# A seven-slot K ring, half-size softmax steps and a turned down projection in a two-layer decode kernel

## The chip, the cores and the metric

The kernel runs on one core of one Trainium2 chip. The metric is the device time of one execution in microseconds (us).

PE is the tensor engine, DVE the vector engine, ACT the scalar engine, SP the engine that only issues the loads here. PSUM is the memory that PE writes to; the kernel uses it as eight banks of 512 float32 columns per partition.

## The reference

One token per sequence is decoded (batch 4, model width 512). The same attention layer and the same feed-forward layer are applied twice, with the same weights and the same caches. Shortened:

```python
# x: (4, 1, 512); k_cache, v_cache: (4, 8, 8192, 128); 32 query heads, 8 K/V heads
# wq: (512, 4096)   wo: (4096, 512)   w_gate, w_up: (512, 1792)   w_down: (1792, 512)   all bfloat16
def attention(x):
    q = (x @ wq).reshape(4, 1, 32, 128).transpose(0, 2, 1, 3)
    k = jnp.repeat(k_cache, 4, axis=1)
    v = jnp.repeat(v_cache, 4, axis=1)
    p = softmax(einsum("bhqd,bhkd->bhqk", q, k) * 128 ** -0.5)
    o = einsum("bhqk,bhkd->bhqd", p, v)
    return o.transpose(0, 2, 1, 3).reshape(4, 1, 4096) @ wo

def ffn(x):
    return (silu(x @ w_gate) * (x @ w_up)) @ w_down

for layer in range(2):                     # written out in the reference
    x = x + attention(layernorm(x))
    x = x + ffn(layernorm(x))
```

## The kernel before

Per layer there are 64 K chunks and then 64 V chunks, each 1 MB: 1024 positions of one K/V head for all four sequences. A K chunk is loaded by SP, transposed by PE in 32 blocks of 128x128 into PSUM "staging" banks, copied out by DVE or ACT, and multiplied with the padded queries (`qk`). After every eight chunks (a range of 1024 positions for all heads) DVE takes a maximum and ACT an exponential. When all 64 chunks are through, `finalize_pt` brings the eight ranges to one common maximum and transposes P; then the V chunks are multiplied (`pv`).

Three things in it matter for the change. The first is where K chunks lie. Four buffers (`kraw`) form a ring. Chunks 4, 5 and 6 lie in the three V buffers, and transposing those releases no load:

```python
    NSK = 4
    NSV = 3
    ...
        VK = (4, 5, 6)
        ring_chunks = [i for i in range(nchunks) if i not in VK]
        NRING = NSK

        def kslot(i):
            if i in VK:
                j = i - VK[0]
                return vbuf[:, j, :, :], f"vb{j}", sem_v[j]
            r = ring_chunks.index(i) % NRING
            if r < NSK:
                return kraw[:, r, :, :], f"kraw{r}", sem_k[r]
            ...
        def ring_next(i):          # the load that transposing chunk i makes possible
            if i in VK:
                return None
            r = ring_chunks.index(i) + NRING
            return ring_chunks[r] if r < len(ring_chunks) else None

        vslot_aps = [vbuf[:, j, :, :] for j in range(NSV)] + wqr_aps   # V: three buffers, then the quarters of wq_sb
```

The second is the use of the PSUM banks. Two pairs hold scores in turn (a pair is a whole range), which leaves four banks for staging:

```python
        stgK_x = [0, 1, 2, 7]
        sc_banks = [["pb3", "pb4"], ["pb5", "pb6"]]
        ...
            def softmax_range(c):          # once per eight chunks
                j = c % 2
                T.op("dve", lambda e: e.tensor_reduce(negm[:, c:c + 1], sc[j][:, :], AX.X, ALU.max, negate=True), ...)
                T.op("act", lambda e: e.activation(pp[:, c * SR:(c + 1) * SR], sc[j][:, :], ACTF.Exp,
                                                   bias=negm[:, c:c + 1], scale=1.0, accum_out=lsum[:, c:c + 1]), ...)
            ...
            def k_loop():
                for i in range(HEAD - 1):
                    qk(i)
                for i in range(HEAD, nchunks):
                    transposes(i)
                    qk(i - 1)
                qk(nchunks - 1)
```

The third is the layer boundary, whose order of issue is also the order of work on PE (in the trace from 369.38 us, the transposes of chunk 0, to 390.25, the Q projection), and the down projection in it:

```python
        def ffn_down():
            for fo in range(FO):                       # 14 matmuls of 512 columns, four rows of output
                bank = MISC - (fo % 2)
                T.op("pe", lambda e: e.matmul(ps[0:B, bank * BANKF:(bank + 1) * BANKF],
                                              lhsT=hT[:, fo * B:(fo + 1) * B], rhs=wd_sb[:, fo, :], ...), ...)

        def ffn_residual():
            for bank in (MISC, MISC - 1):
                T.op("dve", lambda e: e.tensor_tensor(x_sb[:], x_sb[:], ps[0:B, bank * BANKF:(bank + 1) * BANKF], ALU.add), ...)
        ...
        L1["pv"](next_layer=L2)
        L2["prefetch_vk"]()
        ev0 = L2["transposes"](0, banks=[0, 1, 2, 4], defer_evac=True)
        L1["residual"]()
        ffn_up()
        ev0()
        ffn_act(final=False)
        ffn_down()
        ev1 = L2["transposes"](1, banks=[3, 5, 0, 1], defer_evac=True)
        ffn_residual()
        L2["qproj"]()
```

One oddity concerns both kernels alike. Wq is loaded once, V chunks then overwrite its four quarters, and layer 2's Q projection multiplies with what lies there. (The program has a line that loads Wq again, but under `if not last`, which is false for layer 2, the only layer that calls it.) The result still passes the comparison with the reference; why it passes was not tested.

Of the kernel before, what the change touches and what calls it, by code (L numbers as in the profile page):

```python
# [5 lines left out]
ALU = mybir.AluOpType  # L6
# [96 lines left out]
def bass_interleave_layers__gqa_block_cached__swiglu_ffn__decode_kernel(  # L103
# [24 lines left out]
    NCH = S // SR  # L128
    NSK = 4
# [6 lines left out]
    with ExitStack() as es:  # L136
# [24 lines left out]
        negm = sb("negm", [P, NCH], FP32)  # L161
        lsum = sb("lsum", [P, NCH], FP32)
        gnegm = sb("gnegm", [P, 1], FP32)
        dm = sb("dm", [P, NCH], FP32)
        alpha = sb("alpha", [P, NCH], FP32)
        wl = sb("wl", [P, NCH], FP32)
# [8 lines left out]
        hT = sb("hT", [P, FO * B], BF16)  # L175
        xo_bf = sb("xo_bf", [B, D], BF16)
# [9 lines left out]
        stgK = [0, 1, 2]  # L186
        stgK_x = [0, 1, 2, 7]
        stgP = [4, 5, 6]
        sc = [ps[:, 3 * BANKF:5 * BANKF], ps[:, 5 * BANKF:7 * BANKF]]
        sc_banks = [["pb3", "pb4"], ["pb5", "pb6"]]  # L190
# [33 lines left out]

        def act_preload(func):
            T.op("act", lambda e: e.activation(dmy_out[:], dmy_in[:], func), reads=["dmyin"], writes=["dmy"])
# [8 lines left out]
        VK = (4, 5, 6)  # L235
        assert len(VK) <= NSV
        ring_chunks = [i for i in range(nchunks) if i not in VK]

# [3 lines left out]
        NRING = NSK  # L242

        def kslot(i):
            if i in VK:
                j = i - VK[0]
                return vbuf[:, j, :, :], f"vb{j}", sem_v[j]
            r = ring_chunks.index(i) % NRING
            if r < NSK:
                return kraw[:, r, :, :], f"kraw{r}", sem_k[r]  # L250
            j = r - NSK
            return wqr_aps[j], wqr_keys[j], sem_wqr[j]

        def ring_pos(i):
            return None if i in VK else ring_chunks.index(i)

        def ring_next(i):
            if i in VK:
                return None
            r = ring_chunks.index(i) + NRING  # L260
            return ring_chunks[r] if r < len(ring_chunks) else None
# [7 lines left out]
        vslot_aps = [vbuf[:, j, :, :] for j in range(NSV)] + wqr_aps  # L269
        vslot_keys = [[f"vb{j}"] for j in range(NSV)] + [[k] for k in wqr_keys]  # L270
        vsems = sem_v + sem_wqr
# [39 lines left out]
        def make_attention(first, last):  # L311
# [12 lines left out]
            def qproj():  # L324
                layer_norm_T()
# [19 lines left out]
            def transposes(i, banks=None, defer_evac=False):  # L345
# [38 lines left out]
                if nxt == nchunks - 1:  # L384
# [3 lines left out]
                    for v in range(min(nvs, nchunks)):  # L388
                        dma_v(v)

            def softmax_range(c):
                j = c % 2
                T.op("dve", lambda e: e.tensor_reduce(negm[:, c:c + 1], sc[j][:, :], AX.X, ALU.max,  # L393
                                                      negate=True),
                     reads=sc_banks[j], writes=[f"negm{c}"])
                blocks = [f"pp{c * M + m}" for m in range(M)]
                T.op("act", lambda e: e.activation(pp[:, c * SR:(c + 1) * SR], sc[j][:, :], ACTF.Exp,  # L397
                                                   bias=negm[:, c:c + 1], scale=1.0,
                                                   accum_out=lsum[:, c:c + 1]),
                     reads=sc_banks[j] + [f"negm{c}"], writes=blocks + ["lsum"])  # L400

            def qk(i):
                c, g = chunk_coords(i)
                j = c % 2
                for q2 in range(2):
                    for b in range(B):
                        src, skeys = kpiece(i, b)
                        T.op("pe", lambda e: e.matmul(sc[j][32 * b:32 * (b + 1), q2 * 512:(q2 + 1) * 512],  # L408
# [5 lines left out]
                             reads=["qpad"] + skeys, writes=[sc_banks[j][q2]])  # L414
                if g == G - 1:
                    softmax_range(c)

            def k_wq_slots_start():
# [244 lines left out]
```

## Time and profile before

| | before |
|---|---|
| median of the first 6 runs | 748.56 us (747.12 to 750.14) |
| span of the profiled run | 747.0 us |
| read from HBM | 282.33 MB |
| rate in steady stretches | 407 GB/s |
| last V load landed | 725.14 us |

These lines are from the page of the kernel before: the span, the bytes moved in 40 equal slices of it (18.7 us each), the queue of instruction fetches (packets, MB, share), the sum of the reads, and two of the DMA issues (times issued, KB each, median us to landing).

```profile
span 747.0 us, 21812 instructions
...
GB/s 340 406 340 405 388 404 404 393 402 387 395 408 407 407 406 407 406 407 407 410 396 264 279 401 404 405 406 402 400 405 397 407 407 406 408 407 406 407 257 1
...
q8 instruction: 78, 1.28, 0.6%
...
HBM read 282.33 MB, written 0.00 MB: 378 GB/s over the span
...
wq_sb<-in_A_v_cache_dram SPq DMA_DIRECT2D x72, 1024.0 KB, 13.6
...
wq_sb<-in_A_wq_dram SPq DMA_DIRECT2D x1, 4096.0 KB, 17.3
```

Most slices stand at 402 to 408 GB/s, so the load queue is what bounds the kernel nearly all the time. The exceptions are the third slice (340), the two at the layer boundary (264 and 279), and the end. The last two lines are the oddity of Wq: loaded once, with 72 V chunks put into the same tile.

The next lines are the table by stretch of the kernel before. The columns are the stretch and its length, the busy time (and instructions) of PE, PE's weight loads, DVE, ACT and POOL, then the granted PE clock, the share of the DMA engines and GB/s.

```profile
40.00:50.00 10.00, 9.37 (x154) 7.08 (x152) 7.49 (x11) 6.69 (x8) 0.00 (x0) 1.00 0.90 306
...
400.00:410.00 10.00, 8.29 (x139) 6.20 (x140) 5.73 (x13) 3.79 (x4) 0.00 (x0) 1.00 0.66 225
410.00:420.00 10.00, 9.37 (x154) 7.08 (x152) 7.89 (x12) 7.02 (x8) 0.00 (x0) 1.00 0.52 182
420.00:430.00 10.00, 9.72 (x159) 7.54 (x160) 6.14 (x10) 5.92 (x6) 0.00 (x0) 1.00 1.01 355
```

PE is busy for 8.3 to 9.7 us of each ten while the loads stand half still. There the loads wait for PE: in this program a load can only be issued when a buffer has been transposed (SP waited for PE's transposes 257.8 us in all, in 108 waits).

Why PE is late at the boundary is told by the chain of waits of the kernel before (start, duration, what).

```profile
361.69 19.67 DMA wd_sb<-in_B_w_down_dram
381.45 4.80 PE ps L576 x13
...
390.25 3.45 PE ps L328 x128
```

The load of w_down lands at 381.4 us, the down projection takes 4.8 us, and the Q projection of layer 2 can start at 390.25 us.

How fast PE gets through K is seen in the timeline of the kernel before around one softmax (start, duration, engine, line, operation; in brackets the idle time before it and what ended it).

```profile
417.81 1.11 ACT L397 ACTIVATE pp<-ps,negm 128x1024 bf16<-128x1024 f32 x1 [0.91 <-PE ps L359]
...
418.82 0.19 ACT L397 ACTIVATION_READ_ACCUMULATOR pp<-ps,negm 128x1 f32 x1
418.91 1.02 ACT L285 ACTIVATE ktp<-ps 128x1024 bf16<-128x1024 bf16 x1
...
419.98 0.73 PE L359 MATMUL ps<-ident,kraw 128*128 128x128 bf16 x10 [0.63 <-ACT ktp L285]
```

The exponential and its accumulator hold ACT for 1.2 us (417.81 to 419.01); the copy that ACT owes is late; PE has no free staging bank and stops 0.63 us (0.8 us with its weight load). Eight chunks take PE 7 x 2.44 + 3.25 = 20.33 us.

The end of the kernel before, from the timeline:

```profile
725.19 1.04 PE L506 MATMUL ps<-vbuf,pp 128*32 128x128 bf16 x32 [3.03 <-DMA vbuf<-in_A_v_cache_dram]
...
737.87 5.98 PE L576 MATMUL ps<-wd_sb,hT 128*4 128x512 bf16 x14 [1.64 <-DVE hT L571]
743.62 1.39 DVE L583 TENSOR_TENSOR x_sb<-x_sb,ps 4x512 f32<-4x512 f32 x2 [5.80 <-PE ps L576]
```

### The profile page before, as it was taken

Reading aid. Unit: us, or ns where it says so; the run is one execution under the profiler, and the core shown is the slowest. Engines: PE = TensorE matmul, PEld = TensorE weight load, DVE = VectorE, ACT = ScalarE, POOL = GpSimd, SP = SyncE. Lnnn points to the kernel's source line nnn. Section 1 sums busy time; section 2 is a strip of 40 time slices with the busy share of each in tenths; the row PEclk is TensorE's granted clock in tenths of the full one; section 3 lists DMA queues with packets and bytes.
Section 4 is the critical chain, followed back from the end, with each engine's and each line's share of the span. In section 5 each row is a group of like instructions: output and inputs, shape, how many; then the busy total and the mean of one; then the engine's idle time right before and its main releaser. Section 6 shows DMA issues by size and latency. Waiting matters only on the chain.

```text
span 747.0 us, 21812 instructions
## 1 busy us (share of the span) xinstructions
PE 517.6 (69%) x9948; PEld 383.0 (51%) x9948; DVE 278.9 (37%) x466; ACT 232.4 (31%) x258; POOL 1.6 (0%) x11
## 2 busy tenths in 40 slices
PE   3899999999544454444568999999995544445435
PEld 2776777777432333333446777777775333333322
DVE  3376676667500000000234767666664000000002
ACT  3365666566500000000133665656654000000001
POOL 0000000000000000000000000000000000000000
PEclk9799999999855555555578999999998555555555
DMA  8999999999999999999997799999999999999960
GB/s 340 406 340 405 388 404 404 393 402 387 395 408 407 407 406 407 406 407 407 410 396 264 279 401 404 405 406 402 400 405 397 407 407 406 408 407 406 407 257 1
DMA packets 142780, 283.75 MB, mean 380 GB/s; under 512 B 4184, under 2 KB 10080, under 8 KB 142176
## 3 DMA queue, kind: packets, MB, share of 16 engines
q1 hardware_dynamic: 142688, 282.35, 98.7%
q8 instruction: 78, 1.28, 0.6%
q14 instruction: 14, 0.11, 0.0%
HBM read 282.33 MB, written 0.00 MB: 378 GB/s over the span
## 4 chain that ended last, share of the span: by engine, by line
DMA 41%; PE 27%; SPq 21%; DVE 4%; issue 3%; ACT 2%; ACTq 0%; DVEq 0%
SPq L92 21%; PE ps L359 17%; DMA kraw<-in_A_k_cache_dram 15%; DMA wq_sb<-in_A_v_cache_dram 12%; DMA vbuf<-in_A_v_cache_dram 9%; PE ps L408 4%; DMA wd_sb<-in_B_w_down_dram 3%; DMA wq_sb<-in_A_wq_dram 2%; PE ps L506 2%; PE ps L488 2%; DVE negm L393 1%; ACT ktp L285 1%; PE ps L576 1%; PE ps L328 1%; DVE o_red L475 1%
## 5 line engine op out<-in xcount | busy, mean ns | idle before, releaser
L359 PEld LDWEIGHTS ps<-ident,kraw 128*128 128x128 bf16 x3904 | 224.2, 99 | 79.0 <-DMA kraw<-in_A_k_cache_dram 61.6
L359 PE MATMUL ps<-ident,kraw 128*128 128x128 bf16 x3904 | 247.5, 222 | 22.2 <-DMA kraw<-in_A_k_cache_dram 13.2
L283 DVE COPY ktp<-ps 128x1024 bf16<-128x1024 bf16 x310 | 206.7, 688 | 100.4 <-PE ps L359 99.8
L285 ACT ACTIVATE ktp<-ps 128x1024 bf16<-128x1024 bf16 x186 | 183.5, 1021 | 119.7 <-PE ps L359 119.7
L506 PE MATMUL ps<-wq_sb,pp 128*32 128x128 bf16 x2304 | 77.5, 300 | 85.4 <-DMA wq_sb<-in_A_v_cache_dram 84.6
L475 DVE TENSOR_REDUCE o_red<-ps 128x128 f32<-128x384 f32 x16 | 8.9, 557 | 298.3 <-PE ps L506 298.3
L506 PEld LDWEIGHTS ps<-wq_sb,pp 128*32 128x32 bf16 x2304 | 57.0, 132 | 104.1 <-DMA wq_sb<-in_A_v_cache_dram 93.0
L297 ACT ACTIVATE sdv<-mv,eps_sb 4x1 f32<-4x1 f32 x4 | 1.2, 293 | 338.7 <-DVE mv L296 338.7
L506 PE MATMUL ps<-vbuf,pp 128*32 128x128 bf16 x1792 | 58.7, 292 | 65.6 <-DMA vbuf<-in_A_v_cache_dram 65.6
L506 PEld LDWEIGHTS ps<-vbuf,pp 128*32 128x32 bf16 x1792 | 42.8, 129 | 80.2 <-DMA vbuf<-in_A_v_cache_dram 72.4
L408 PE MATMUL ps<-ktp,qpad 128*32 128x512 bf16 x992 | 76.4, 384 | 3.8 <-DVE qpad L340 3.4
L488 PE MATMUL ps<-wo_sb,oT_sb 128*4 128x512 bf16 x64 | 29.9, 621 | 5.1 <-DVE oT_sb L486 5.1
L408 PEld LDWEIGHTS ps<-ktp,qpad 128*32 128x32 bf16 x992 | 15.6, 94 | 17.7 <-DVE qpad L340 3.8
L397 ACT ACTIVATE pp<-ps,negm 128x1024 bf16<-128x1024 f32 x16 | 17.8, 1113 | 18.2 <-DVE negm L393 15.5
L393 DVE TENSOR_REDUCE negm<-ps 128x1 f32<-128x1024 f32 x16 | 19.6, 1224 | 6.9 <-PE ps L408 6.9
L283 DVE COPY pp<-ps 128x1024 bf16<-128x1024 bf16 x20 | 13.4, 688 | 20.6 <-PE ps L359 17.3
L285 ACT ACTIVATE pp<-ps 128x1024 bf16<-128x1024 bf16 x12 | 12.1, 1023 | 20.3 <-PE ps L359 16.4
L460 PE MATMUL ps<-ident,pp 128*128 128x128 bf16 x128 | 11.6, 273 | 8.1 <-DVE pp L451 7.9
L483 PE MATMUL ps<-ident,o_accb 128*128 128x128 bf16 x16 | 4.6, 288 | 16.7 <-DVE o_accb L480 14.8
L460 PEld LDWEIGHTS ps<-ident,pp 128*128 128x128 bf16 x128 | 10.8, 127 | 9.6 <-DVE pp L451 8.9
L576 PE MATMUL ps<-wd_sb,hT 128*4 128x512 bf16 x28 | 11.0, 575 | 5.3 <-DMA wd_sb<-in_B_w_down_dram 3.6
L488 PEld LDWEIGHTS ps<-wo_sb,oT_sb 128*4 128x4 bf16 x64 | 5.6, 108 | 17.5 <-issue 9.5
(58 smaller groups left out, 114.1 us busy)
## 6 DMA issues: line engine op xcount, KB each, us to landing
kraw<-in_A_k_cache_dram SPq DMA_DIRECT2D x122, 1024.0 KB, 8.2
wq_sb<-in_A_v_cache_dram SPq DMA_DIRECT2D x72, 1024.0 KB, 13.6
vbuf<-in_A_v_cache_dram SPq DMA_DIRECT2D x56, 1024.0 KB, 13.5
vbuf<-in_A_k_cache_dram SPq DMA_DIRECT2D x6, 1024.0 KB, 14.2
wq_sb<-in_A_wq_dram SPq DMA_DIRECT2D x1, 4096.0 KB, 17.3
wo_sb<-in_A_wo_dram SPq DMA_DIRECT2D x1, 4096.0 KB, 18.5
wg_sb<-in_B_w_gate_dram SPq DMA_DIRECT2D x1, 1792.0 KB, 15.1
wu_sb<-in_B_w_up_dram SPq DMA_DIRECT2D x1, 1792.0 KB, 16.9
```

What stands on the lines that cost most here:

```text
L92: ins = self.eng[engname].dma_start(out_ap, in_ap)
L283: T.op("dve", lambda e: e.tensor_copy(dst, src), reads=reads, writes=writes)
L285: T.op("act", lambda e: e.activation(dst, src, ACTF.Copy), reads=reads, writes=writes)
L359: T.op("pe", lambda e: e.matmul(stg[:, t * P:(t + 1) * P], lhsT=kap[:, b, t * Dh:(t + 1) * Dh], rhs=ident[:], is_transpose=True, start=Tru ...
L393: T.op("dve", lambda e: e.tensor_reduce(negm[:, c:c + 1], sc[j][:, :], AX.X, ALU.max, negate=True), reads=sc_banks[j], writes=[f"negm{c}"])
L397: T.op("act", lambda e: e.activation(pp[:, c * SR:(c + 1) * SR], sc[j][:, :], ACTF.Exp, bias=negm[:, c:c + 1], scale=1.0, accum_out=lsum[: ...
L408: T.op("pe", lambda e: e.matmul(sc[j][32 * b:32 * (b + 1), q2 * 512:(q2 + 1) * 512], lhsT=qpad[:, b, g, :], rhs=src[:, q2 * 512:(q2 + 1) * ...
L460: T.op("pe", lambda e: e.matmul(stg[:, t * P:(t + 1) * P], lhsT=pp[:, blk * P:(blk + 1) * P], rhs=ident[:], is_transpose=True, start=True, ...
L475: T.op("dve", lambda e: e.tensor_reduce(o_red[:], src, AX.X, ALU.add), reads=keys, writes=["ored"])
L488: T.op("pe", lambda e: e.matmul(ps[0:B, OPJ * BANKF:(OPJ + 1) * BANKF], lhsT=oT_sb[:, bass.ds(h, B, step=Hq)], rhs=wo_sb[:, h, :], start=( ...
L506: T.op("pe", lambda e: e.matmul(ps[32 * b:32 * (b + 1), bank * BANKF: bank * BANKF + Dh], lhsT=pp[:, blk * P + 32 * b: blk * P + 32 * (b + ...
L576: T.op("pe", lambda e: e.matmul(ps[0:B, bank * BANKF:(bank + 1) * BANKF], lhsT=hT[:, fo * B:(fo + 1) * B], rhs=wd_sb[:, fo, :], start=(fo ...
```

## The change

It has six parts, named here for the experiments.

- A, the ring: seven K slots (four `kraw`, three `vbuf`), every transposed chunk releases a load; V starts in the quarters of `wq_sb` and goes to `vbuf` as K leaves it.
- B, the start: Wq is loaded first, and the Q projection comes ahead of the transposes.
- C, the softmax: per 512 columns, in one pair of score banks instead of two, so that staging gets six banks instead of four.
- D, the boundary: w_gate and w_up are loaded ahead of K chunk 0, and chunk 0 of layer 2 is transposed after the activation of the feed-forward layer.
- E, the down projection turned: w_down becomes the stationary operand, 56 matmuls of four columns, then a copy, four transposes and one addition.
- F, 40 dummy transposes at the start of `finalize_pt`, meant to keep PE's granted clock from falling while it waits (in the kernel before it was 0.50 from 562.67 us, while PE waited 3.96 us until 564.16 us for the scaling of P).

The core of the diff:

```diff
+    QB = SR // 512
+    NBLK = NCH * QB
...
-        stgK_x = [0, 1, 2, 7]
-        sc = [ps[:, 3 * BANKF:5 * BANKF], ps[:, 5 * BANKF:7 * BANKF]]
-        sc_banks = [["pb3", "pb4"], ["pb5", "pb6"]]
+        stgK_x = [0, 1, 2, 5, 6, 7]
+        SCB = 3
...
+        NRING = NSK + NSV
-        ring_chunks = [i for i in range(nchunks) if i not in VK]
         def kslot(i):
-            if i in VK:
-                j = i - VK[0]
-                return vbuf[:, j, :, :], f"vb{j}", sem_v[j]
-            r = ring_chunks.index(i) % NRING
+            r = i % NRING
             if r < NSK:
                 return kraw[:, r, :, :], f"kraw{r}", sem_k[r]
+            return vbuf[:, r - NSK, :, :], f"vb{r - NSK}", sem_v[r - NSK]
         def ring_next(i):
-            ...
+            return i + NRING if i + NRING < nchunks else None
...
-        vslot_aps = [vbuf[:, j, :, :] for j in range(NSV)] + wqr_aps
+        vslot_aps = wqr_aps + [vbuf[:, j, :, :] for j in range(NSV)]
...
-                    for v in range(min(nvs, nchunks)):
+                    for v in range(NSK):
                         dma_v(v)
+                if i >= nchunks - NRING and i % NRING >= NSK:
+                    dma_v(i % NRING)
...
+            def softmax_block(k):
+                bank = SCB + (k % QB)
+                scb = ps[:, bank * BANKF:(bank + 1) * BANKF]
+                ...   # as before, on 512 columns: negm[:, k], pp[:, k * 512:(k + 1) * 512], lsum[:, k]
...
             def finalize_pt():
+                pe_warm(40)
...
                     if v + nvs == nv - 1:
+                        if first:
+                            T.dma("sp", wg_sb[:], ...)
+                            T.dma("sp", wu_sb[:], ...)
                         if next_layer is not None:
                             dma_k(0)
                         if first:
-                            T.dma("sp", wg_sb[:], ...)
-                            T.dma("sp", wu_sb[:], ...)
                             T.dma("sp", wd_sb[:], ...)
...
         def ffn_down():
-            for fo in range(FO):
-                ...   # 14 matmuls of 512 columns
+            for nq in range(NQ):
+                for fo in range(FO):
+                    T.op("pe", lambda e: e.matmul(misc[:, nq * B:(nq + 1) * B],
+                                                  lhsT=wd_sb[:, fo, nq * P:(nq + 1) * P],
+                                                  rhs=hT[:, fo * B:(fo + 1) * B], ...), ...)
+            T.op("dve", lambda e: e.tensor_copy(ffT[:], misc[:, 0:NQ * B]), ...)
+            for nq in range(NQ):
+                T.op("pe", lambda e: e.matmul(bank6_bf[0:B, nq * P:(nq + 1) * P], lhsT=ffT[:, nq * B:(nq + 1) * B],
+                                              rhs=ident[:], is_transpose=True, ...), ...)
...
-        dma_k(0)
-        dma_k(1)
         T.dma("sp", wq_sb[:], A_wq...)
-        dma_k(2)
-        dma_k(3)
+        for i in range(NSK):
+            dma_k(i)
-        L1["transposes"](0)
-        L1["transposes"](1)
         L1["qproj"]()
-        L1["transposes"](2)
-        L1["transposes"](3)
         L1["qpad_fill"]()
+        for i in range(HEAD):
+            L1["transposes"](i)
...
-        ev0 = L2["transposes"](0, banks=[0, 1, 2, 4], defer_evac=True)
         L1["residual"]()
         ffn_up()
-        ev0()
         ffn_act(final=False)
+        ev0 = L2["transposes"](0, banks=[0, 1, 2, 4], defer_evac=True)
         ffn_down()
+        ev0()
```

## The prediction

> **What bounds the kernel now.** The load queue. The page counts 282.3 MB of HBM reads; in steady stretches the slices run at 407 GB/s, so pure transfer is 694 of the 747 us span. By 10 us stretches (view of busy time by stretch), the remaining 53 us are: 3.5 us before and during the first loads; 6.4 us of dips in layer 1's K phase (306 GB/s at 40-50 us, then scattered); 13.5 us at the layer boundary (357, 225, 182, 355 GB/s from 390 to 430 us); about 1.5 us later in layer 2; 25 us of tail after the last V load (from about 722 us).
>
> **Why it dips.** K has a ring of four slots; chunks 4-6 sit in the three V buffers, and transposing them releases no load. At the boundary SP has issued K up to chunk 10; chunk 11 waits until chunk 7 is transposed (413.5 us). The tensor engine sets that time: the chain is wd landing (381.4), down projection (4.8), residual, layer norm, Q projection (390.3), K transposes. It cannot catch up much: a K chunk costs 2.44 us (timeline), plus a 0.8 us stop once per eight chunks, where ACT's 1024-column exponential (1.11 + 0.19 us) delays an eviction and the four staging banks run out: 20.3 us per eight chunks, against 20.6 us for their loads.
>
> **What changes.**
> 1. Ring of seven slots: every transposed chunk releases a load. Wq moves ahead of K; the Q projection should start near 14 instead of 19.5 us, chunk 4 near 29 instead of 32. Layer 1's K dips should nearly go: 5.5 us.
> 2. Softmax per 512 columns in one pair of banks, so six staging banks. The score banks lose their double buffer, but half reductions (about 0.63 us, estimated from 1.22) and half exponentials should be done before the next range's first scores, one chunk of transposes later. The 0.8 us stop should mostly vanish; the tensor engine then runs at 2.45 us a chunk and catches up.
> 3. Boundary: wu lands one K chunk (2.6 us) earlier, but wd does not, and still gates the down projection. Turned around, that is 56 small matmuls; the up projection's 56 of the same shape took 1.6 us (28 ns each), plus a copy and four transposes (0.8 us), in place of 4.8 us; one addition of 0.68 us goes. Q projection about 3 us earlier. With ring and faster K loop, 10-13 of the 13.5 us return.
> 4. Tail: 737.9 to 745.0 us shrinks by 3.9 us, all on the chain.
> 5. The 40 dummy transposes fit the 4 us in which PE waits for softmax scaling. [...] About 1 us, mostly hidden.
>
> V phases stay at 407 GB/s: no gain.
>
> **Sum.** 5.5 + 12 + 1 + 3.9 = 22 us: **726 us**, range 719 to 736. Faster by over 2% (below 733.6): 0.80; within: 0.18; slower: 0.02.
>
> **What would show it.** Slices of GB/s without dips at 40 and 400 us; last load ending near 704 us; the tail after it 21 us; about 19.5 us per eight chunks where data is there; down projection under 3 us.
>
> **What would make it wrong.** The single score buffer stalls PE (over 1.1 us per eight chunks makes PE the limit: gain only 8-10 us); PV of layer 2 cannot start earlier, so the seven V slots fill and the boundary gap merely moves; SP's in-order issue holds the boundary chain.

The sum is 5.5 + 12 + 1 + 3.9 = 22.4 us, given as 22. The 1 us of step 5 was the author's estimate. What the trace of the kernel before shows: in layer 1, 48 transposes of P take 4.27 us from 194.52 us (89 ns each), with the granted clock at 0.50 until 197.44 us; 32 transposes of the K loop, at 187.07 us, take 1.96 us (61 ns each) at 1.00. The 0.8 us for a copy and four transposes in step 3 was an estimate too; in the kernel after they take 0.81 us at the end (724.09 to 724.90 us).

## More of the kernel before

From the start of the last V chunk's matmuls to the end of the span it is 21.8 us, of which the down projection and its two additions are 7.1 us.

## The result, and the profile after

The changed kernel is correct and takes 729.97 us (median of 8 runs, 728.8 to 731.1) against 748.62 us for the kernel before in the same rounds (16 runs). The ratio is 0.9747, with a 95% interval of 0.9735 to 0.976: faster by 2.5%. Ratios here are the mean time of one kernel's fast runs over the mean of the other's fast runs in the same rounds, so they are not quite the ratios of the medians quoted.

The same lines of the page, for the kernel after (slices of 18.2 us):

```profile
span 727.7 us, 22112 instructions
...
GB/s 344 405 406 406 407 407 404 407 406 402 387 408 407 406 407 407 407 401 406 411 379 396 397 407 405 405 406 405 406 406 362 399 407 407 406 406 407 408 342 2
...
q8 instruction: 79, 1.29, 0.6%
```

The hollow of the third slice is gone and that of the boundary nearly so (379 GB/s at the least). A smaller one is new: the 31st slice, 362, which is the start of layer 2's V phase. The table by stretch, kernel after, columns as before:

```profile
40.00:50.00 10.00, 9.71 (x160) 7.52 (x158) 7.75 (x12) 7.14 (x11) 0.00 (x0) 1.00 1.05 405
...
400.00:410.00 10.00, 9.71 (x164) 7.68 (x160) 7.85 (x13) 6.63 (x10) 0.00 (x0) 1.00 1.05 391
410.00:420.00 10.00, 10.00 (x164) 7.71 (x164) 6.72 (x11) 6.66 (x7) 0.00 (x0) 1.00 1.05 405
420.00:430.00 10.00, 9.71 (x164) 7.70 (x160) 7.84 (x13) 6.65 (x10) 0.00 (x0) 1.00 1.05 404
550.00:560.00 10.00, 5.91 (x213) 5.29 (x211) 5.46 (x14) 5.19 (x7) 0.00 (x0) 1.00 0.87 325
```

At the boundary, from the timeline of the kernel after, the down projection takes 1.64 us, starts 5.3 us earlier than before, and the Q projection follows at 382.80:

```profile
376.16 1.64 PE L578 MATMUL ps<-hT,wd_sb 128*128 128x4 bf16 x56 [1.20 <-issue]
...
382.80 3.58 PE L327 MATMUL ps<-xnT,wq_sb 128*128 128x4 bf16 x128 [0.28 <-DVE xnT L307]
```

One softmax of the kernel after, from its timeline:

```profile
409.05 0.69 ACT L399 ACTIVATE pp<-ps,negm 128x512 bf16<-128x512 f32 x1
...
409.28 0.40 PE L410 MATMUL ps<-ktp,qpad 128*32 128x512 bf16 x4
...
409.63 0.19 ACT L399 ACTIVATION_READ_ACCUMULATOR pp<-ps,negm 128x1 f32 x1
...
409.97 0.40 PE L410 MATMUL ps<-ktp,qpad 128*32 128x512 bf16 x4 [0.29 <-DVE ktp L281]
```

A stop is left, but another one. The first four score matmuls of the next range run at 409.28, and the second four must wait until ACT has read the second score bank (409.63 + 0.19 = 409.82). The bracket names DVE, but the copy that it means (ended at 409.85) belongs to a later K chunk. That the wait is for ACT follows from the order of the program, and e5_three_score below confirms it: a third score bank takes away this wait alone, and the stop is gone. Eight chunks now take 19.98 us instead of 20.33.

The end of the kernel after, from its timeline:

```profile
709.71 1.04 PE L505 MATMUL ps<-wq_sb,pp 128*32 128x128 bf16 x32 [1.51 <-DMA wq_sb<-in_A_v_cache_dram]
...
722.40 1.65 PE L578 MATMUL ps<-hT,wd_sb 128*128 128x4 bf16 x56 [1.64 <-DVE hT L570]
724.09 0.17 DVE L583 CAST ffT<-ps 128x16 bf16<-128x16 f32 x1 [1.75 <-PE ps L578]
724.32 0.58 PE L585 MATMUL ps<-ident,ffT 128*4 128x128 bf16 x4 [0.27 <-DVE ffT L583]
724.94 0.68 DVE L590 TENSOR_TENSOR x_sb<-x_sb,ps 4x512 f32<-4x512 f32 x1 [0.68 <-PE ps L585]
```

The last stretch before it, kernel after, by single microseconds (columns of the table by stretch):

```profile
704.00:705.00 1.00, 0.37 (x16) 0.37 (x20) 0.00 (x0) 0.00 (x0) 0.00 (x0) 0.50 0.94 356
705.00:706.00 1.00, 0.68 (x28) 0.41 (x16) 0.00 (x0) 0.00 (x0) 0.00 (x0) 0.50 0.55 213
706.00:707.00 1.00, 0.00 (x0) 0.00 (x0) 0.00 (x0) 0.00 (x0) 0.00 (x0) 0.50 0.51 199
707.00:708.00 1.00, 0.85 (x32) 0.78 (x32) 0.00 (x0) 0.00 (x0) 0.00 (x0) 0.50 0.50 195
```

The loads do not end at once. From 705 us they run at about half the rate for three microseconds and then at less (80 GB/s from 708 to 709), until the last V chunk lands at 709.67 us. This plateau, which is there before the change too but shorter, turned out to be the key to what the prediction had missed.

Where the 19.3 us between the two profiled spans came from, by milestones read from the two traces (us from the start of the span):

| milestone | before | after | earlier by |
|---|---|---|---|
| last addition of layer 1's PV | 366.56 | 361.74 | 4.8 |
| Q projection of layer 2 starts | 390.25 | 382.80 | 7.5 |
| K done in layer 2 (common maximum) | 561.50 | 547.03 | 14.5 |
| first PV matmul of layer 2 | 570.41 | 555.67 | 14.7 |
| last V load lands | 725.14 | 709.67 | 15.5 |
| end of the span | 747.0 | 727.7 | 19.3 |

So layer 1 gave 4.8 us, the boundary and layer 2 gave 10.7 us more, and the tail gave 3.8 us.

### The profile page after: what moved, and what is told of

It is laid out like the page before. It is cut to its first block, busy times and chain, and to the rows that moved or that the text cites. A ratio compares the mean times of both kernels' runs of the same rounds, so it can differ in the third digit from the quotient of the medians.

```text
span 727.7 us, 22112 instructions
## 1 busy us (share of the span) xinstructions
PE 510.3 (70%) x10120; PEld 386.6 (53%) x10120; DVE 280.4 (39%) x494; ACT 237.4 (33%) x293; POOL 1.6 (0%) x11
## 3 DMA queue, kind: packets, MB, share of 16 engines
q8 instruction: 79, 1.29, 0.6%
## 4 chain that ended last, share of the span: by engine, by line
DMA 38%; PE 32%; SPq 21%; DVE 5%; issue 3%; ACT 0%; ACTq 0%; DVEq 0%
SPq L92 21%; PE ps L358 19%; DMA wq_sb<-in_A_v_cache_dram 14%; DMA kraw<-in_A_k_cache_dram 10%; DMA vbuf<-in_A_v_cache_dram 10%; PE ps L410 5%; DMA vbuf<-in_A_k_cache_dram 4%; PE ps L505 3%; PE ps L487 2%; DVE ktp L281 1%; DVE o_red L474 1%; DVE o_accb L479 1%; PE ps L482 0%; PE ps L327 0%; DVE negm L395 0%
## 5 line engine op out<-in xcount | busy, mean ns | idle before, releaser
L358 PEld LDWEIGHTS ps<-ident,kraw 128*128 128x128 bf16 x2368 | 139.9, 101 | 31.5 <-DMA kraw<-in_A_k_cache_dram 17.8
L358 PE MATMUL ps<-ident,kraw 128*128 128x128 bf16 x2368 | 152.2, 225 | 3.2 <-DMA kraw<-in_A_k_cache_dram 2.2
L358 PEld LDWEIGHTS ps<-ident,vbuf 128*128 128x128 bf16 x1728 | 96.6, 98 | 24.8 <-DMA vbuf<-in_A_k_cache_dram 12.9
L358 PE MATMUL ps<-ident,vbuf 128*128 128x128 bf16 x1728 | 105.8, 219 | 2.0 <-DMA vbuf<-in_A_k_cache_dram 1.2
L410 PE MATMUL ps<-ktp,qpad 128*32 128x512 bf16 x992 | 78.9, 385 | 5.7 <-DVE ktp L281 3.2
L410 PEld LDWEIGHTS ps<-ktp,qpad 128*32 128x32 bf16 x992 | 17.2, 94 | 23.3 <-DVE ktp L281 8.4
L399 ACT ACTIVATE pp<-ps,negm 128x512 bf16<-128x512 f32 x32 | 22.0, 687 | 8.3 <-DVE negm L395 5.6
L395 DVE TENSOR_REDUCE negm<-ps 128x1 f32<-128x512 f32 x32 | 20.6, 686 | 3.4 <-PE ps L410 3.4
L459 PE MATMUL ps<-ident,pp 128*128 128x128 bf16 x128 | 8.3, 220 | 6.7 <-DVE pp L281 3.8
## 6 DMA issues: line engine op xcount, KB each, us to landing
vbuf<-in_A_v_cache_dram SPq DMA_DIRECT2D x54, 1024.0 KB, 13.5
```

Source lines behind the costliest of these rows:

```text
L358: T.op("pe", lambda e: e.matmul(stg[:, t * P:(t + 1) * P], lhsT=kap[:, b, t * Dh:(t + 1) * Dh], rhs=ident[:], is_transpose=True, start=Tru ...
L395: T.op("dve", lambda e: e.tensor_reduce(negm[:, k:k + 1], scb, AX.X, ALU.max, negate=True), reads=[f"pb{bank}"], writes=[f"negm{k}"])
L399: T.op("act", lambda e: e.activation(pp[:, k * 512:(k + 1) * 512], scb, ACTF.Exp, bias=negm[:, k:k + 1], scale=1.0, accum_out=lsum[:, k:k ...
L410: T.op("pe", lambda e: e.matmul(ps[32 * b:32 * (b + 1), bank * BANKF:(bank + 1) * BANKF], lhsT=qpad[:, b, g, :], rhs=src[:, q2 * 512:(q2 + ...
L459: T.op("pe", lambda e: e.matmul(stg[:, t * P:(t + 1) * P], lhsT=pp[:, blk * P:(blk + 1) * P], rhs=ident[:], is_transpose=True, start=True, ...
```

## The experiments

The first question was which part of the change pays. The theory before was that the ring pays only together with a faster K loop and an earlier boundary chain; the rival, that the ring is nearly everything. The second question came from the first answers: the last load still landed 5.7 us after the 704 us that the prediction had named, so what are these microseconds? Twelve kernels ran. The median of the kernel before lay between 748.2 and 748.5 us in their rounds; a ratio's interval is about 0.001 to 0.002 to either side, that is 1 to 1.5 us, and differences below that are called unresolved.

| run | edit | median us | ratio (95%) | last V landing us |
|---|---|---|---|---|
| after | all six parts | 729.97 | 0.9747 (0.9735 to 0.976) | 709.67 |
| e1_ring_only | before + A | 739.72 | 0.9883 (0.9866 to 0.99) | 717.76 |
| e12_old_ring | after - A | 735.7 | 0.9826 (0.9807 to 0.9845) | 716.65 |
| e2_old_softmax | after - C | 731.32 | 0.9768 (0.9746 to 0.979) | 710.9 |
| e3_old_down | after - E | 733.14 | 0.9797 (0.9775 to 0.9818) | 709.25 |
| e4_no_warm | after - F | 730.7 | 0.9761 (0.9742 to 0.9779) | 711.62 |
| e8_old_boundary | after - D | 730.15 | 0.9757 (0.9741 to 0.9773) | 709.92 |
| e9_old_start | after - B | 730.1 | 0.9754 (0.9738 to 0.977) | 710.08 |
| e5_three_score | after, no softmax stop | 730.3 | 0.9762 (0.9748 to 0.9775) | 710.25 |
| e6_more_v | after, eleven V slots once | 729.21 | 0.975 (0.9737 to 0.9764) | 709.46 |
| e7_both | e5 and e6 together | 729.25 | 0.9746 (0.9733 to 0.9759) | 709.28 |
| e11_loads_only | after, loads alone | 699.8 | 0.935 (0.9335 to 0.9365) | 695.9 |
| e13_reload_wq | after, Wq loaded twice | 740.03 | 0.9888 (0.9867 to 0.9909) | 721.76 |

The last column is read from one profiled execution each. Layer 1's last PV addition already lies between 361.7 and 363.0 us in the variants of the kernel after, so differences of a microsecond in this column should not be read as effects of an edit.

### The ring alone

Part A was put into the kernel before; all else stayed.

```diff
# against the kernel before
-        NRING = NSK
+        NRING = NSK + NSV
-            (K chunks 4 to 6 apart, ring of four)
+            (kslot, ring_next, vslot_aps and the first V loads as in the change)
```

> The kernel before with the seven-slot K ring and the new order of V slots alone. My theory (the tensor engine's pace limits what the ring gives back at the layer boundary): the dip at 40 to 50 us goes, the last PV of layer 1 ends 4 to 5 us earlier; in layer 2 the K loop stays at 20.3 us per eight chunks and is limited by the tensor engine throughout, PV of layer 2 starts only 6 to 8 us earlier than before; total about 741 us (739 to 743). Rival (the ring is the whole of it, because the loop has slack): boundary dip gone too, total about 733 us.

It measured 739.72 us, a gain of 8.8 us of the 18 to 19. The table by stretch of this run tells why not more:

```profile
400.00:410.00 10.00, 10.00 (x171) 7.66 (x164) 5.43 (x8) 5.29 (x6) 0.00 (x0) 1.00 0.87 302
410.00:420.00 10.00, 9.37 (x154) 7.08 (x152) 7.25 (x11) 6.63 (x8) 0.00 (x0) 1.00 1.02 360
...
560.00:570.00 10.00, 8.04 (x273) 7.62 (x270) 3.35 (x6) 4.55 (x5) 0.00 (x0) 0.79 0.61 194
```

Where the kernel before has 225 and 182 GB/s at the boundary, there are now 302 and 360. But at 560 to 570 us a hollow of 194 GB/s has come up. PE is no faster, so K of layer 2 ends at 555.5 us, the V slots fill up before the first PV matmul at 564.7 us, and part of the gap has only moved from the start of layer 2's K phase to its end. This is the case that the prediction named under "what would make it wrong". (Two milestones of my expectation came short: layer 1 ended 3.6 us earlier, not 4 to 5, and PV of layer 2 started 5.7 us earlier, not 6 to 8.)

### All but the ring

```diff
# against the kernel after: part A undone
-            r = i % NRING
+            if i in VK:
+                j = i - VK[0]
+                return vbuf[:, j, :, :], f"vb{j}", sem_v[j]
+            r = ring_chunks.index(i) % NRING
   (ring_next, vslot_aps and the first V loads as in the kernel before)
```

> The changed kernel with the four-slot ring and V slots of before, everything else new. My theory (the ring is needed, but also the faster tensor engine behind it): the standstill at 40 us in layer 1 and the one at the boundary come back, the latter shorter than before because the chain to the Q projection is shorter; total 8 to 11 us over the changed kernel (738 to 741 us), so that the ring alone (8.8 us) and the rest alone (8 to 10 us) add up to about the whole. Rival (the ring and the rest do the same thing twice): 734 us or less.

It measured 735.7 us, about 5.8 us over the kernel after: less than the 8 to 11 us expected, and more than the rival's 4. The hollow at the boundary is back, in the table by stretch of this run:

```profile
400.00:410.00 10.00, 10.00 (x166) 7.74 (x164) 7.85 (x13) 6.41 (x9) 0.00 (x0) 1.00 0.54 177
```

The hollow at 40 to 50 us is not (403 GB/s there), although the old ring made part of it in the kernel before: I read this as the work of the earlier start and the faster K loop, which let PE empty the old ring in time; no run takes these two apart.

The ring alone gains 8.8 us, all the rest alone 12.5 us, both together 18.7 us (medians, each against the kernel before in its own rounds). The sum of the two is 2.6 us larger than the whole, hardly more than the intervals allow. This alone is no sign of a floor. In the last landings the ring alone gains 7.4 us, the rest alone 8.5 us and both together 15.5 us, so up to the last load the two parts add up.

### The softmax

```diff
# against the kernel after: part C undone
-        stgK_x = [0, 1, 2, 5, 6, 7]
-        SCB = 3
+        stgK_x = [0, 1, 2, 7]
+        sc_banks = [["pb3", "pb4"], ["pb5", "pb6"]]
-                        softmax_block(c * QB + q2)
+                    softmax_range(c)
```

> The changed kernel with softmax per 1024 columns, double score banks and four staging banks as before. My theory (layer 2's K loop is limited by the tensor engine, and the split takes 0.35 us off each of its eight stops): 20.3 us per eight chunks in layer 2 instead of 20.0, PV of layer 2 starts 2.5 to 3 us later, total about 2.5 us over the changed kernel (732.5 us); layer 1 unchanged, since loads limit it. Rival (the tensor engine has slack in both layers): no difference within 0.5 us.

The K loop of layer 2 became 2.5 us longer, as expected. But the total rose by 1.6 us only (by the ratios), which the intervals don't separate from nothing, and the last V load landed 1.2 us later. Of the 2.5 us, 0.6 us were given back in `finalize_pt` (eight ranges instead of sixteen blocks) and 1 us by a boundary that ran earlier in this run, so the first PV matmul came 0.9 us later than in the kernel after. The mechanism of part C is right, and its worth in time is small.

### The down projection

```diff
# against the kernel after: part E undone
-            for nq in range(NQ):
-                for fo in range(FO):            # 56 matmuls of four columns, a copy, four transposes
+            for fo in range(FO):                # 14 matmuls of 512 columns into two banks
-            (one addition)
+            (two additions)
```

> The changed kernel with the old down projection. My theory: the tail after the last V chunk grows by 3.8 us; at the boundary the chain to the Q projection grows by 2 to 3 us, and since the tensor engine limits layer 2's K loop, that passes through: total 5.5 to 7 us over the changed kernel (about 736 us). Rival (only the tail counts, the boundary part is hidden behind loads): 3.8 us over.

It cost 3.2 us against the kernel after by the medians (3.7 us by the ratios), which is about the tail alone: the time after the last landing is 21.5 us here and 18.0 us in the kernel after. I had expected 5.5 to 7 us, with the boundary's share, so the total speaks for the rival. But the profile shows that this run does not test what the rival says of the boundary. The granted clock was full there (1.00 from 375.15 to 385.39 us, where the kernel after had 0.50 until 390.7), so the old down projection took 3.18 us and not 4.8 as in the kernel before (granted clock 0.61 in the mean), and the transposes behind it 1.96 us and not 3.60 as in the kernel after (0.50):

```profile
376.21 3.18 PE L575 MATMUL ps<-wd_sb,hT 128*4 128x512 bf16 x14 [1.31 <-issue]
...
379.33 1.96 PE L358 MATMUL ps<-ident,kraw 128*128 128x128 bf16 x32
```

The Q projection of layer 2 therefore started only 0.4 us later than in the kernel after, and K was done 0.85 us later; the last V load landed at 709.25 us, not later. So a delay of 0.85 us did not show in the last landing. Whether the three microseconds of the prediction would have is not shown.

### The dummy transposes

```diff
# against the kernel after
             def finalize_pt():
-                pe_warm(40)
```

> The changed kernel without the 40 dummy transposes. My theory: the 64 real transposes after softmax run at about 89 ns instead of 60, PV of layer 2 starts 1 to 1.5 us later, and because the seven V slots are full by then (the load queue stood still for about 2 us there), the total rises by 1 to 1.5 us; layer 1 hides it. Rival (hidden in both layers): same within 0.3 us.

The total rose by 0.7 us, unresolved. In the profiled execution the first PV matmul of layer 2 came 2.6 us later and the last load landed at 711.62 us, 2.0 us later, but 1.1 us of that was there before the boundary (w_down landed at 377.16 us, in the kernel after at 376.07). The transposes themselves are clearer. These are the transposes of P, first in the kernel after and then in this run, from the groups of instructions (busy us, mean ns of one, idle before and its causes).

```profile
L459 PE MATMUL ps<-ident,pp 128*128 128x128 bf16 x128 | 8.3, 220 | 6.7 <-DVE pp L281 3.8 <-DVE pp L451 2.5 <-ACT pp L283 0.4
```

```profile
L458 PE MATMUL ps<-ident,pp 128*128 128x128 bf16 x128 | 12.8, 290 | 9.8 <-DVE pp L450 7.1 <-DVE pp L281 2.7
```

With the dummies the 128 transposes take 8.3 us, without 12.8 us, and the way from the common maximum to the first PV matmul of layer 2 is 8.64 us against 10.28 us. In the kernel after the granted clock stays at 1.00 until 561.37 us, without the dummies it falls to 0.50 at 551.71. The dummies are no guarantee, though: in e6_more_v, which has them, it fell at 552.85 us.

What sets the moment at which the clock changes is not shown. At the boundary of the kernel after PE is without a break on the Q projection and the transposes from 382.80 us, and the clock stays at 0.50 until about 390.7 us, nearly 8 us. The first 3.4 us of it are matmuls of only four columns; from the first transpose of 128 columns at 386.24 us it is 4.5 us, and in e3_old_down, from 386.48 to 392.21, 5.7 us. The moment varies between the runs: before 386 us the kernel after had 0.50 throughout, e2_old_softmax 1.00 at 376 to 378 and at 382 to 384 us, and e3_old_down 1.00 from 375.15 to 385.39 us.

### Boundary order and start order

```diff
# e8_old_boundary, against the kernel after: part D undone
-                            (w_gate and w_up loaded ahead of K chunk 0)
+                            (w_gate and w_up loaded behind K chunk 0)
+        ev0 = L2["transposes"](0, banks=[0, 1, 2, 4], defer_evac=True)
         L1["residual"]()
         ffn_up()
+        ev0()
         ffn_act(final=False)
-        ev0 = L2["transposes"](0, banks=[0, 1, 2, 4], defer_evac=True)
         ffn_down()
-        ev0()
```

> The changed kernel with the boundary order of before (chunk 0 of K loaded before the gate and up weights, its transposes before the layer norm). My theory (wd gates the down projection in both orders, so the order is worth little): Q projection of layer 2 within 1 us of the changed kernel's, total within 1 us of it. Rival (the earlier up weights are worth their 2.6 us): about 2 us over.

```diff
# e9_old_start, against the kernel after: part B undone
+        dma_k(0)
+        dma_k(1)
         T.dma("sp", wq_sb[:], ...)
-        for i in range(NSK):
-            dma_k(i)
+        dma_k(2)
+        dma_k(3)
   (and two transposed chunks ahead of the Q projection again)
```

> The changed kernel with the start of before (two K chunks ahead of Wq, transposes of chunks 0 and 1 ahead of the Q projection). My theory (with seven slots the start matters little, because the loads are continuous as soon as every transposed chunk releases one): Q projection at 19.5 us instead of 13.6, but no standstill at 40 us; total within 1.5 us of the changed kernel. Rival (the early Q projection is what fills layer 1's dips): 3 us or more over.

Both stayed within 1 us of the kernel after (730.15 and 730.1 us), as expected. In e8_old_boundary the Q projection started at 382.73 us, as in the kernel after: the load of w_down gates this chain in both orders (it landed at 376.00 and 376.07 us, and the down projection started 0.09 us later in both).

### The stop and the standstill that were left

Two visible faults were left in the kernel after: the 0.46 us stop per softmax, and the hollow at 550 to 560 us, where all seven V slots are full and the loads stand still. Both can be taken away. A third score bank lets the next range begin without waiting for ACT:

```diff
# e5_three_score, against the kernel after
-        stgK_x = [0, 1, 2, 5, 6, 7]
+        stgK_x = [0, 1, 2, 6, 7]
+        NSC = 3
-                bank = SCB + (k % QB)
+                bank = SCB + (k % NSC)
```

> The changed kernel with three score banks in rotation and five staging banks (two and six before). My theory (what is left of the stop per softmax, 0.46 us, is the next range's second score group waiting for the second half exponential, since both score banks are in use): 19.5 to 19.6 us per eight chunks in layer 2 while data is there, gnegm of layer 2 about 3 us earlier, the dip of the load queue at the start of PV of layer 2 (2 us) gone, total 1.5 to 2 us under the changed kernel (about 728 us). Rival (the stop is eviction: too few staging banks): no shorter stop, or a longer one, and no gain.

And four idle K buffers can each take one V chunk, so that eleven V chunks are on their way before the first PV matmul:

```diff
# e6_more_v, against the kernel after
-                if i >= nchunks - NRING and i % NRING >= NSK:
-                    dma_v(i % NRING)
+                if i >= nchunks - NRING:
+                    dma_v(NSK + i - (nchunks - NRING))
   (V chunks 4 to 10 take the slot of the K chunk that has just been transposed)
```

> The changed kernel in which the four idle K buffers take four V chunks once, so that eleven V chunks instead of seven can be in flight when PV starts. My theory (the 2 us standstill at the start of PV of layer 2 is full V slots behind a late tensor engine): standstill gone although PV starts at the same time, total 1.5 to 2.5 us under the changed kernel (about 728 us). Rival (the standstill has another cause, such as instruction fetch beside the data): no change.

The third run of this group has both edits in one kernel.

```diff
# e7_both, against the kernel after
+        NSC = 3                                          (and the rest of e5_three_score)
+                    dma_v(NSK + i - (nchunks - NRING))   (and the rest of e6_more_v)
```

> Three score banks and eleven V slots together. My theory (both remove the same standstill, after which the load queue alone is the limit): no better than the better of the two by more than 0.5 us, about 727.5 us. Rival (independent causes): 3 to 4 us under the changed kernel.

The edits worked, with one exception. In e5_three_score eight chunks take 19.58 us; its second group of scores follows the first without a stop, all eight in one piece, in the timeline:

```profile
429.92 0.61 PE L411 MATMUL ps<-ktp,qpad 128*32 128x512 bf16 x8
```

But K of layer 2 was done at 547.4 us, as in the kernel after (547.0), and not 3 us earlier: in this execution the K loop began 1 us later, and PE now waited 1.1 us for loads. So the hollow stayed (341 GB/s at 550 to 560 us), and this run tests the stop alone.

In e6_more_v the hollow is gone; two stretches of it show no standstill, where the kernel after had 325 GB/s in the first:

```profile
550.00:560.00 10.00, 7.07 (x208) 6.63 (x206) 5.17 (x13) 5.01 (x6) 0.00 (x0) 0.83 1.05 409
560.00:570.00 10.00, 6.08 (x170) 4.45 (x170) 1.07 (x3) 0.00 (x0) 0.00 (x0) 0.66 1.05 403
```

In e7_both it is gone too (406 GB/s in both stretches). And none of the three gained: 730.3, 729.21 and 729.25 us, all within the noise of the kernel after. My expectation of 1.5 to 2 us failed. The last landings are at 710.25, 709.46 and 709.28 us, where the kernel after has 709.67. In e6_more_v the end of the loads looks like this:

```profile
704.00:705.00 1.00, 0.75 (x32) 0.75 (x32) 0.00 (x0) 0.00 (x0) 0.00 (x0) 0.50 0.54 207
705.00:706.00 1.00, 0.30 (x12) 0.03 (x4) 0.00 (x0) 0.00 (x0) 0.00 (x0) 0.50 0.52 203
706.00:707.00 1.00, 0.00 (x0) 0.00 (x0) 0.00 (x0) 0.00 (x0) 0.00 (x0) 0.50 0.53 207
```

The full rate ends before 704 us, a microsecond or more earlier than in the kernel after. But the half-rate plateau that follows is the longer for it, and the last load lands where it did. The mean rate had gone up, and the time had not come down.

### The loads alone

So the question became what holds the last load back. In the traces each load raises its semaphore in 16 steps, here called its completions, and PE's matmuls on it start after the last of them (in the kernel after the last completion is at 709.67 us, the matmuls start at 709.71). In the kernel after the first and the last of the 16 lie up to 6.1 us apart before the hollow and 4.7 to 4.8 us in the last seven loads. Of the last load eight completions come from 705.00 to 705.50 us and the other eight from 708.01 to 709.67. So the half rate at the end, 203 of 407 GB/s, falls where eight of the sixteen completions have come and eight are still to come. I read the completions as those of the 16 DMA engines that the page counts, one each; the trace does not name the engine of a completion.

My theory was that some DMA engines are slower by themselves, which would let even the bare loads land no earlier than 706 us; the rival, that they are held up by something the kernel does.

```diff
# against the kernel after: every load in its order, no other instruction; the result is wrong on purpose
+        real_op = T.op
+        T.op = lambda *x, **k: None
...
-        T.op("dve", lambda e: e.tensor_copy(xo_bf[:], x_sb[:]), reads=["x"], writes=["xo"])
+        real_op("dve", lambda e: e.tensor_copy(xo_bf[:], xb_sb[:]), reads=["xb"], writes=["xo"])
+        for sm in sem_k + sem_v + sem_wqr + list(sem_w.values()):
+            if T.semval.get(id(sm)):
+                nc.sync.wait_ge(sm, T.semval[id(sm)])
```

> The changed kernel's loads alone, in the same order into the same slots, each waiting for the load before it in its slot; no engine computes, and the result is wrong on purpose. All of the last eight kernels have their last V chunk landed at 709.3 to 711.6 us, whether the load queue stood still on average or not, and in their traces the sixteen completions of one load lie up to 5.5 us apart: the slowest of the sixteen goes at 2.60 to 2.63 us a chunk in the V phases, the fastest at 2.57. My theory now (the changed kernel has reached the pace of the slowest channels, and my 694 us was the mean of all sixteen): last landing at 706 to 710 us, span 708 to 712 us. Rival (my account of the prediction: 407 GB/s can be had to the end, 12 us are still lost to waits): last landing at 697 to 700 us.

The result is wrong, as meant (relative error 0.9993). The last load landed at 695.9 us, so my theory fell and the rival held, even a little below its range of 697 to 700. From the page of this run:

```profile
span 697.9 us, 300 instructions
```

And its last stretches, in the table by stretch (DVE, POOL, PE clock, DMA share, GB/s):

```profile
692.00:694.00 2.00, 0.00 (x0) 0.00 (x0) 1.00 1.05 410
694.00:696.00 2.00, 0.00 (x0) 0.00 (x0) 1.00 0.23 87
```

There is no plateau: the rate is full until 694 us (410 GB/s), and the sixteen completions of the last load lie within 1.3 us of each other. Without the rest of the kernel the bytes landed in 696 us. What the kernel adds is computing, waits and, by the page, 22,112 instructions with 79 packets (1.29 MB) in the queue of instruction fetches, where this run has 300 instructions and none in that queue.

In the traces of the kernel after and of e6_more_v I then followed the spread of each load's completions (the last of the 16 against the fourth). It does not grow evenly. It jumps, and ten of the jumps fall together with every eighth packet of the queue of instruction fetches. Worked out from the trace of the kernel after:

```
time of jump, us    spread grows by, us    fetch packets so far
  22.8                1.26                   1
  85.8                1.34                   9
 153.9                1.44                  17
 227.8                1.39                  25
 311.2                1.37                  33
 390.3                1.07                  41
 455.9                1.15                  49
 518.8                1.14                  57
 582.0                0.64                  65
 663.0                0.65                  73
```

Late in the run three more jumps of 0.7 to 0.9 us stand between these (at 64, 68 and 76 packets), where the late completions are no longer level with each other. In e6_more_v the ten jumps stand at the same counts, within 0.1 us of these times, with 0.88 to 1.42 us each. The fetches of this kernel are packets of 16,384 bytes that last about 0.93 us each, 79 of them (a second instruction queue has 14 of 8,192 bytes). The reading that fits, an inference and not a measurement, is that they go round eight of the sixteen DMA engines, one each, so that each of the eight falls behind by about 1.2 us per round (the mean of the ten lines is 1.15), while the other eight do not. The steps between two jumps look like the round itself: after 1, 2, 4, 6 and 8 fetch packets, 1, 2, 4, 6 and 8 of a load's sixteen completions are within half a microsecond of the last, and the ninth packet puts one far behind again. In the other kernels the jumps come eight packets apart too, in some as two interleaved series (in the kernel before at 7, 15, 23, 31 and at 18, 26, 34, 42). The spread falls where the loads slow down for a moment: in the kernel after by 1.2 us at 195.6 us, by 1.5 at 378.7 and by 4.1 at 562.5, the hollow.

The loads alone hold a test of this. That run computes nothing and fetches nearly nothing, but two instruction packets of 8,192 bytes fall into it, at 207.45 and 541.77 us. After each of them one completion of the sixteen is late for good, by 0.46 us from the load that lands at 209.82 us and by 0.66 us more from the one at 544.60. Nowhere else in the run does the spread (first to last, 0.30 to 0.45 us in the hundred microseconds before the first packet) change by more than 0.25 us from one load to the next. So after each of these instruction packets one completion was late with no computing beside it, and by about half (0.46 and 0.66 us) of what goes with a packet of twice the size in the list above (1.07 to 1.44 us in its first eight lines).

For the kernel after, ten rounds make 11.5 us by the list, or 12.7 us at the mean of its first eight lines (1.27 us). Added to the bare loads this is an estimate of 707.4 to 708.6 us for the earliest last landing. The kernel after has 709.67 us, e6_more_v 709.46, e7_both 709.28, e3_old_down 709.25.

By this reading a standstill of the mean rate costs less than it looks: the engines that are ahead stand still, and those that are behind go on with loads already issued. What the traces show of it is the hollow. In the kernel after the load that lands at 559.94 us has its completions 5.90 us apart, and the next one, at 562.50 us, 1.48: the completions that were ahead have lost their lead. In e6_more_v, without a hollow, it is 5.93 and 6.03 us, yet the loads at the same two places land at 560.03 and 562.70 us, no earlier.

The size of the floor remains an estimate. e11_loads_only took away computing, waits and nearly all fetches at once, and no run took away the fetches alone (a kernel with the same work in fewer instructions). That test stays open.

### Loading Wq again

```diff
# against the kernel after: a second load of Wq, ahead of layer 2's Q projection
+                T.dma("sp", wq_sb[:], A_wq.rearrange("(kt p) n -> p kt n", p=P), sem_w["wq"],
+                      writes=["wq"] + wqr_keys)
   (and the line under `if not last`, which never ran, is taken out)
```

> The changed kernel with Wq loaded a second time before layer 2's Q projection. In the kernel before and in the changed one the profile shows one load of Wq and then 72 and 74 V chunks into the same buffer, so that layer 2 projects with V data; the check passes because the scores are small. Expected: correct as before, 4.2 MB more at 407 GB/s, 10.3 us, and some stop of the tensor engine while it waits for Wq: 11 to 20 us over the changed kernel.

It is correct and takes 740.03 us, 10.1 us more than the kernel after: the 4 MB at 407 GB/s are 10.3 us. That is just below the 11 to 20 us expected: the Q projection of layer 2 started 11.5 us later (394.34 us), but no more than the transfer shows in the total. With the weights that the reference means in layer 2, the changed kernel would still be 1.1% faster than the kernel before is without them.

No version was faster than the changed kernel beyond the noise. Taken out one at a time, the parts A, E, C, F, D and B cost 5.7, 3.2, 1.4, 0.7, 0.2 and 0.1 us by the medians; only the first two are clear of it.

## Why the prediction was right or wrong

The prediction, 726 us with a range of 719 to 736 and 0.80 for faster by over 2%, was right in direction, in class and in range; the measured median of 729.97 us is 4 us above its centre. As its sum has it, against the spans of the two profiled runs:

| step | predicted, us | measured, us |
|---|---|---|
| 1: start and layer 1 (ring, start order) | 5.5 | 4.8 |
| 2, 3 and 5: K loop, boundary, dummy transposes, to the last landing | 12 + 1 | 10.7 |
| 4: tail | 3.9 | 3.8 |
| sum | 22.4 | 19.3 |

**Step 1** was right in mechanism and nearly in size. The Q projection starts at 13.64 us (predicted 14), chunk 4 at 28.61 us (predicted 29), and the stretch from 40 to 50 us has 405 GB/s.

**Step 2** was half right. The stop of 0.8 us fell to 0.46, not to nearly nothing, because the second score bank is still being read when PE wants it; eight chunks take 19.98 us where about 19.5 were predicted. e5_three_score shows that the rest of this stop costs nothing that can be measured: without it PE waits for loads instead.

**Step 3**: the Q projection came 2.6 us earlier relative to the end of layer 1 (23.7 to 21.1 us; predicted about 3), and w_down gates the chain as said. What the turned projection gave at the boundary by itself stays open: in e3_old_down a faster clock kept the chain within 0.4 us of the kernel after. What pays at the boundary is the ring together with the rest (e1_ring_only, e12_old_ring).

**Step 4** was right: 21.8 to 18.0 us after the start of the last PV chunk.

**Step 5** was right: 8.3 us of transposes instead of 12.8 in e4_no_warm, and in the total no more than 0.7 us, unresolved.

**The term that was mis-sized** is in step 3, "10-13 of the 13.5 us return", with the 1 us of step 5. It measured 10.7 us in place of 13. It rested on the first paragraph, "pure transfer is 694 of the 747 us span", which takes each standstill of the mean rate as time that can be had back. The bare loads do land at 695.9 us. But in this kernel, with its 79 fetch packets, the sixteen completions of a load come up to 6.1 us apart, and the last load lands at about 707.4 us at the earliest, by the estimate above. So "last load ending near 704 us" was below that floor, if the estimate holds; it ended at 709.67. The same paragraph took the end of the loads before as "about 722 us", where the rate falls off, while the last of the sixteen completions came at 725.14 us; its tail of 25 us was 21.8. e5_three_score removes the stop, e6_more_v the standstill and e7_both both, which seemed to be the missing microseconds, and their last loads land at 710.25, 709.46 and 709.28 us.

Of what the prediction named as dangers, "the boundary gap merely moves" is what happens with the ring alone (194 GB/s at 560 to 570 us in e1_ring_only), and in small in the kernel after (325 GB/s at 550 to 560 us).

## What to carry to other kernels

The deeper ring gave 8.8 us with the old pace of PE behind it and 18.7 us with the other parts, and alone it left a hollow of 194 GB/s at 560 to 570 us: look where the standstill goes to, not only where it leaves. The mean rate times the bytes, 694 us, was not the floor of this kernel; look at the last of a load's sixteen completions, run the loads alone (695.9 us here), and count the instructions of the unrolled program, since here ten jumps of the completions, 11.5 us in all, came with every eighth of their fetches. Before a run is read as the test of one part, look in its trace whether that part's own time changed as meant: in e3_old_down another clock hid the very difference that was to be tested.
